# A two-layer transformer kernel whose matrix order is planned at build time: transposed P stored by layer in two halves, planner durations replaced, and the order written out anew

## The chip, the cores and the metric

The kernel runs on one core of one Trainium2 chip. A core has a matrix engine (TensorE, PE in the profile, with its weight loads shown apart as PEld), a vector engine (VectorE, DVE), a scalar engine (ScalarE, ACT), a general engine (GpSimd, POOL) and a queue engine (SyncE, SP) that starts most transfers. The metric is the device time of one execution in microseconds.

## What is computed

Two layers A and B are applied twice to x (2048 rows of 576, bf16). A is attention over segments of 32 rows with 8 memory rows that the segment before hands on, so its 64 segments are a chain; B is a gated feed-forward layer.

```python
for s in range(n_seg):                      # 64 segments, each needs mem of the one before
    h = concat([mem, xs])                   # 8 + 32 rows
    q, k, v = h @ Wq, h @ Wk, h @ Wv        # 576 -> 32 heads of 128
    p = softmax(where(mask, q @ k.T * scale, -1e9))
    o = (p @ v) @ Wo
    mem = o[:M]; outs.append(o[M:])
...
x = x + A(layernorm(x)); x = x + B(layernorm(x))     # B: (silu(x@w1) * (x@w3)) @ w2, 576 -> 4608 -> 576
x = x + A(layernorm(x)); x = x + B(layernorm(x))
```

## The kernel before, in words

The two applications of A run interleaved. Step t works on segment t of the first application and on segment t - 8 of the second (`LAG`), so that in the middle most matrix instructions serve both: 80 columns, 40 of each layer. There are 72 steps; the first 8 and the last 8 have one layer alone ("one-layer steps", 40 columns), and the 56 between have two. Every fourth step a feed-forward job of 128 rows per layer starts, whose pieces are laid between the attention work.

A step has four head groups g of 8 heads. For a group, TensorE's work is a chain of blocks, each with a letter in the written order:

- Q and q: queries and keys (32 matmuls over 128 rows of the contraction, and 8 short ones for its last 64 rows, the "tail"). ScalarE or VectorE moves the result from PSUM into tile QKT.
- S: scores. VectorE adds the mask, takes the maximum, subtracts, ScalarE takes the exponential (tile SME), VectorE sums, inverts and multiplies into tile PB (3 or 4 instructions).
- T: transposes P, 8 matmuls from PB through the small matrix `fold`, whose 320 result columns (8 heads by 40) are shared by both layers on different partitions. Two evictions then read the same PSUM bank whole and write tile PTS, one for each layer, each multiplied by a column of zeros and ones (`slots`) that keeps the partitions of its layer. Each goes to ScalarE or VectorE, as the planner chooses (`pt_ev`, line 1022). There is one PTS buffer.
- P: 8 matmuls, V by PTS, 80 columns each (`pv`, line 1039). It needs both evictions, and V. The result is moved to tile OT.
- O and o: output projection, 32 matmuls and 8 for the tail.
- V, v, X, x, G, g: values (memory rows, segment rows, and both of two steps at once), moved to tile V. F, f, W, w: the feed-forward blocks, up (16 and 4 matmuls) and down (8, w for the second layer). a, b, n, p, m: transposes.

The order of everything is fixed when the program is built. `make_nodes` makes one node for each block and each piece of work of another engine, with a duration in microseconds. `plan` (line 76) goes through them: TensorE takes its nodes exactly as the string `ORDER` says (line 222: `FIRST`, eleven times `FOUR`, `LAST`; `FOUR` is 4 steps and 224 letters), and the other engines take whichever ready node can begin first by the durations, which also decides between ScalarE and VectorE where a node may go to either ("AD"), and which PSUM bank and buffer it gets. Only the resulting order is emitted, each engine's instructions chained in that order; the durations are no part of the program. A node is ready some latency after its producers (`PE_LAT`, `EW_LAT`). The planner knows no dependence between the two evictions of one T: both wait for T alone (line 404).

TensorE blocks have modes: whole array ("full"), 64-column halves ("col", where each matmul is issued as two halves side by side, `mm`, line 586), and row or quarter modes for tails. Blocks that may run in either of two modes take that of their neighbours.

Of the kernel before, what the change touches and what calls it, by code (L numbers as in the profile page):

```python
# [13 lines left out]
P = 128  # L14
# [18 lines left out]
PE_LAT = 0.22  # L33
EW_LAT = 0.135
# [17 lines left out]
class Node:  # L52
# [3 lines left out]
    def __init__(self, eng, dur, fn, deps=(), prio=0.0, mode=None, acq=(), rel=(), name="", lat=None):  # L56
        self.eng, self.dur, self.fn, self.prio, self.mode = eng, dur, fn, prio, mode.split("/") if mode else mode
        self.deps = [d for d in deps if d is not None]
        self.acq, self.rel, self.name = list(acq), list(rel), name
        self.lat = lat if lat is not None else (PE_LAT if eng == "PE" else EW_LAT)  # L60
        self.outs, self.ready, self.start, self.end, self.by = [], 0.0, None, None, None
        self.left = len(self.deps)
# [13 lines left out]
def plan(nodes, pools, letters):  # L76
# [42 lines left out]
    while len(order) < len(nodes):  # L119
# [35 lines left out]
        for s in n.acq:  # L155
# [4 lines left out]
            f[s.i] = NOW  # L160
        for s in n.rel:
            s.users -= 1
            s.end = max(s.end, n.end + (PE_LAT if e == "PE" else EW_LAT))
            if s.users == 0:
                free[s.pool][s.i] = s.end
        for m in n.outs:
            m.ready = max(m.ready, n.end + (0.0 if m.eng == e == "PE" else n.lat))
# [8 lines left out]
def actc(*ns):  # L176

    return sum(max(0.067 + n * 0.000833, 0.19) for n in ns)


def dve(*ns):
    return sum(max(0.065 + n / 960.0, 0.19) for n in ns)


def dveh(*ns):

    return sum(max(0.065 + n / 1920.0, 0.19) for n in ns)
# [6 lines left out]
def ewh(*ns):  # L194
# [5 lines left out]
    "amQQQQqqqqSSqqQQQTSQqqSxXVvPTPTOPOOTooPoOoQQqqqqQSQvqqSVQQqTqSQPQOSToPXTOPTxoPOOooQqqqQQSVvqQQSQqqqQSqTQPOSTPTOP"  # L200
    "OToooPaOoQQqqqqQQSvSVQqqqQQQSqTPSXTOPTOPoTxoPOOooQQpQqqqvVqSnQQSFfqFQqfqqQTQSPFTfSOFPWOToPFToffPOOooWQqqqqQQSQQS"
    "FFfqfVvqTQWQqSFxffqQFPSXTWfPFTOPOTOPFOooooWQfqqqQQSFqfqVvQQSFfqTQPWQSqqfFTQOSfoPFTOPWFTOPooffOoFQqqQqqvSQQWSVqqf"
    "FQQWqqSTQPQSTOPabOTXPooTOPxxOooXqqpQQQqqSQnVvfSFTQqqqQQPSFffqQFTOPoSWTFfPOOTFPWOooofQQqfqqFSQFqqfgQGWTQPQSfqFQQq"
    "fqFSWTGFSggfGPGTOPOTfgFaPOOooooWVvqqfQQFFQSqfqQWQSqqfFQTQQqfqSFPWTSFPOTfoOPFWTOPffFOoooWQQqqqqQSbQQQqgqSGSTGPQTq"
    "gqQPOggSGTGPOTOPoooOoQqqqpQVpSQnQvqqqQnQFSTffqFQQPqSwTFPSffOOWTFPFTOPWOoooowFffqqQQQWSfqqFQwQSFqfqgGTQQPWfqSTFFg"
    "gfqGQwPGTOoSPFgfOGTOPWOoooFqqfqQQQQvSwqVSFqqfQQWwTFPQfqfqFTQSwPWSfFOTFPWwOTffFPOOaooooWQQqqqqQwSbQGQgqqSQTQPQqqg"
    "SGTSGPGggTOPOTOPoooOo"
# [5 lines left out]
LAST = (  # L213
    "QqqqpQQQSnpQQqqqVSvTSnQFffqPFOQqTwPoSWTFPffFTOOWPwOoooFFqfqQQQqqfSQQwQfqqFTSGSqfgQFPWQgfqGTSFPGFTfggOOPGTOPwWOoo"
    "ooFFqffqQQwQWQSqqVSvqqQQTFQPSfqqQwTOWSPFTFPofOTOPwOoooWFfqfqQQQQqfqSFwWvVSFTfqqQQPWQqqSvTQVSPOTbOPwOTooPoxOoXqQp"
    "pVvQqqqQSQQnqqSQnqQFTSfqQPFTSOPfTFOPwTOPWOooooFqfqfQQQSVqqqvQQQwSfqFWTFPSfqqQTQOPSFTwfFPOTOPWOooooFfqqQQQSqfxvVX"
    "qfFQwWTSQFQqqqfQPWSTwFPffqQFTWSOwFPffOFTOPwOooooWFvqfqQQQSWqqVQwSFfqqfQFTQQSqqWPQTPSOoTOPwOToobPxOoXqqqQQQpvSVqQ"
    "qQSnqQFfSTQFPqqfQOTSFfPwTOoofPFTOPFOfoowQqqQFSQfqqqQQSVvqqfQFTQFSfqPQOTowPSFTfxXPOTOPFOooowVvqqQQQSqqfQQSqqfQFST"
    "QQPwqqFTSOfPFTOfPwTOPfoooOoFQQqqqqQSQQSqqQVvSfTFPqQQwqfTSFPOTOFPTOPfoooOoFpwnfffFFwFwfffFFFwfffFFwFwfffFFFwfffFF"
# [12 lines left out]
def make_nodes(em, nseg, pools, o=Opt, dma_bw=230e3, load_bw=400e3):  # L232
# [44 lines left out]
    def ln_nodes(tag, src, xn, deps, prio, writes, warm=False):  # L277

        a = node("DVE", 1.16, em.ln_stats(src, xn), deps=deps, prio=prio, acq=[] if src is xn else [xn], name=tag + "stats")
        p_ = node("POOL", 0.45, em.ln_pow(xn), deps=[a], prio=prio, name=tag + "pow")  # L280
        c = node("DVE", 0.46 if src is xn else 0.66, em.ln_norm(src, xn), deps=[p_], prio=prio, name=tag + "norm")
# [28 lines left out]
    def v_nodes(name, t, k, prio, tail_at, emit, strips, deps, tail_deps, free):  # L310
# [6 lines left out]
        for r in (0, 1):  # L317
            outs = em.v_parts(strips, r)
            b[r].users = len(outs)
            for p0, width, row, blk in outs:  # L320
                e = node("AD", (0.55, 0.6), em.v_ev(b[r], p0, width, row, blk), deps=[m_, n] + free.get(blk // 2, []), prio=prio + 0.01 * (blk // 2),
# [19 lines left out]
    def vg_out(t, g, b, deps, row):  # L341

        return [node("AD", (0.55, 0.6), em.v_ev(b[r], row, R64, row, 2 * g + r), deps=deps, prio=t + o.vm + 0.01 * g + (0.05 if row == 0 else 0.0), rel=[b[r]],
# [11 lines left out]
    def step(t):  # L355
# [17 lines left out]
        for g in range(NG):  # L373
# [18 lines left out]
            sc = node("PE", 8 * (0.0165 * nl if nl == 2 else 0.029), em.scores(t, g, qs, s), deps=qe, prio=pf + o.sc, mode="col" if nl == 2 else "full/col", acq=[s, sme], rel=qs, name="SC")  # L392
            a = node("DVE", dve(320), em.sm_add(t, g, s, sme), deps=[sc], prio=pf, rel=[s], name="add")
            m_ = node("DVE", dve(320, 320) + 0.13, em.sm_max(t, g, sme), deps=[a], prio=pf, name="maxsub")
            c = node("ACT", 0.105 + 320 * 0.000833, em.sm_exp(t, g, sme), deps=[m_], prio=pf, name="exp")
            pb = Slot("pb")
            d = node("DVE", dve(320) + 0.2, em.sm_sum(t, g, sme), deps=[c], prio=pf, name="sum")
            w = 0.168 * (4 - e if nl == 2 else 2) + nl * 320 / 960
# [954 lines left out]
```

## Time and profile before

| | |
|---|---|
| time of 3 runs, median (lowest to highest) | 2731.85 us (2730.61 to 2734.94) |
| span of the profiled execution, first to last instruction | 2722.1 us |
| median of the runs less that span | 9.75 us |
| granted TensorE clock, mean over the span | 0.996 |
| VectorE busy | 2115.9 us, 78% |
| ScalarE busy | 1377.2 us, 51% |
| GpSimd busy | 333.4 us, 12% |
| transfers | 322.07 MB, mean 118 GB/s |

The profiled execution's own time outside the span is not recorded, so sums below are made on the span, and the 9.75 us are added at the end. In the profile a row of a group reads: line, engine, operation, tile written <- tiles read, shape, count | busy us, mean ns of one | idle us of that engine just before them, and who ended it. Busy is the union of the bars; a matmul's bar is much longer than the distance to the next matmul, since they are pipelined. Line 591 is the helper that records every matmul, 594 ScalarE's, 597 VectorE's. A row of the timeline reads: start us, length us, engine, line, operation, tiles, shape, count, and in brackets the idle time before it and what ended it.

### The profile page before, as it was taken

The page shows a single profiled execution, that of the slowest core. Times are in us where ns is not written, and L with a number is a line of the kernel's source. Part 1 is how long each engine was busy: PE and PEld are TensorE (multiplying, and loading weights), DVE is VectorE, ACT ScalarE, POOL GpSimd, SP SyncE. Part 2 cuts the span into 40 slices and gives each one's busy share as a digit, 9 for nine tenths or more (in the row PEclk, how much of TensorE's full clock was granted, in tenths as well). Part 3 has the DMA queues.
Part 4 walks back from the last instruction along what each step waited for, and adds up shares of the span by engine and source line. Part 5 has one row for each costly group of instructions (what it writes and reads, how often), then busy time and mean ns, then how long its engine had stood idle before and what let it go on. Part 6 is the DMA issues. An engine that isn't in the chain of part 4 may idle for free.

```text
span 2722.1 us, 136659 instructions
## 1 busy us (share of the span) xinstructions
PE 2629.0 (97%) x60933; PEld 2278.8 (84%) x60933; DVE 2115.9 (78%) x5487; ACT 1377.2 (51%) x3914; POOL 333.4 (12%) x411
## 2 busy tenths in 40 slices
PE   5999999999999999999999999999999999999998
PEld 4788888888888888888888888888888888888886
DVE  5787887887778778777877877787787778687876
ACT  2655554454545455454545545454454545455453
POOL 1111110110111011011101101110110111011110
PEclk8999999999999999999999999999999999999999
DMA  9064524343342334434233433423344342434457
GB/s 314 5 183 122 151 73 126 88 118 116 103 124 84 109 96 118 116 100 124 86 110 96 118 116 98 125 85 111 97 118 116 98 125 71 124 97 121 125 172 252
DMA packets 478176, 322.07 MB, mean 118 GB/s; under 512 B 26024, under 2 KB 467760, under 8 KB 476944
## 3 DMA queue, kind: packets, MB, share of 16 engines
q1 hardware_dynamic: 474048, 305.43, 37.9%
q8 instruction: 477, 7.82, 1.2%
q0 software_dynamic: 3024, 6.93, 0.9%
q10 hardware_dynamic: 512, 0.94, 0.2%
q14 instruction: 115, 0.94, 0.1%
HBM read 308.49 MB, written 2.36 MB: 114 GB/s over the span
## 4 chain that ended last, share of the span: by engine, by line
PE 78%; DVE 10%; ACT 6%; DMA 2%; issue 2%; SPq 1%; ACTq 0%; DVEq 0%
PE bank L591 78%; DVE HTT L597 3%; ACT PTS L594 2%; DVE PTS L597 2%; DVE STAT L597 2%; DVE PB L597 2%; ACT V L594 2%; SPq L600 1%; DVE V L597 1%; DVE SME L597 1%; DMA W<-in_A_Wk_dram 1%; ACT SME L594 1%; DMA W<-in_B_w_dram 1%; DMA WO<-in_A_Wo_dram 0%; ACT QKT L594 0%
## 5 line engine op out<-in xcount | busy, mean ns | idle before, releaser
L591 PEld LDWEIGHTS <-W 128*128 128x128 bf16 (+2 forms) x32064 | 1266.0, 100 | 124.6 <-issue 60.2
L591 PE MATMUL bank<-HT,W 128*128 128x80 bf16 (+3 forms) x23040 | 807.6, 197 | 18.5 <-ACT HT L594 5.7
L591 PE MATMUL bank<-XTB,W 128*64 128x256 bf16 (+5 forms) x9024 | 664.0, 263 | 5.7 <-DMA W<-in_B_w_dram 2.8
L594 ACT ACTIVATE QKT<-bank 128x64 bf16<-128x64 f32 (+2 forms) x1476 | 342.5, 314 | 354.9 <-PE bank L591 350.1
L1010 POOL MEMSET PB<- 128x1024 bf16 x288 | 273.9, 951 | 1922.6 <-PE bank L591 1649.7
L591 PE MATMUL bank<-OT,WO 128*128 128x80 bf16 (+3 forms) x11520 | 409.7, 198 | 4.6 <-ACT V L594 2.2
L591 PEld LDWEIGHTS <-WO 128*128 128x128 bf16 (+1 forms) x11520 | 379.6, 102 | 29.9 <-issue 17.5
L594 ACT ACTIVATE V<-bank 32x512 bf16<-32x512 f32 (+1 forms) x613 | 344.4, 585 | 101.8 <-PE bank L591 94.8
L591 PE MATMUL bank<-WV,HT 128*32 128x512 bf16 (+4 forms) x3680 | 375.8, 381 | 2.1 <-DVE OT L597 0.9
L591 PE MATMUL bank<-W2C,HTT 128*64 128x288 bf16 (+1 forms) x3040 | 320.5, 286 | 2.0 <-DMA W2C<-in_B_w_dram 1.3
L597 DVE TENSOR_REDUCE STAT<-SME 104x8 f32<-104x320 f32 (+1 forms) x576 | 274.5, 477 | 35.1 <-ACT SME L594 29.4
L597 DVE TENSOR_TENSOR PB<-SME,STAT 40x128 bf16<-40x128 f32 (+4 forms) x912 | 274.4, 335 | 9.0
L594 ACT ACTIVATE HTT<-bank 128x512 bf16<-128x512 f32 (+1 forms) x324 | 177.5, 557 | 183.6 <-PE bank L591 182.4
L591 PEld LDWEIGHTS <-HT 128*32 128x32 bf16 (+4 forms) x3680 | 157.1, 99 | 122.0 <-issue 21.0
L591 PEld LDWEIGHTS <-HTT 128*64 128x64 bf16 (+1 forms) x3104 | 227.7, 104 | 35.5 <-issue 2.3
L597 DVE SCALAR_TENSOR_TENSOR XR<-bank,XR 128x288 f32<-128x288 f32 x576 | 239.6, 446 | 13.5 <-PE bank L591 11.6
L597 DVE CAST QKT<-bank 128x192 bf16<-128x192 f32 (+4 forms) x572 | 154.5, 316 | 121.2 <-PE bank L591 120.4
L597 DVE SCALAR_TENSOR_TENSOR HTT<-HTT,bank 128x512 bf16<-128x512 bf16 (+1 forms) x324 | 201.9, 623 | 52.5 <-ACT HTT L594 48.0
L594 ACT ACTIVATE PTS<-bank,slots 128x320 bf16<-128x320 f32 x303 | 151.0, 525 | 163.0 <-PE bank L591 113.7
L597 DVE TENSOR_TENSOR HTT<-HTT,bank 128x512 bf16<-128x512 bf16 (+1 forms) x324 | 203.6, 628 | 29.0 <-DVE HTT L597 0.9
L594 ACT ACTIVATE OT<-bank 128x320 bf16<-128x320 f32 (+1 forms) x402 | 149.6, 403 | 137.7 <-PE bank L591 132.2
L594 ACT ACTIVATE SME<-SME 104x320 f32<-104x320 f32 (+1 forms) x288 | 135.0, 469 | 156.3 <-DVE SME L597 154.5
(69 smaller groups left out, 1847.0 us busy)
## 6 DMA issues: line engine op xcount, KB each, us to landing
W<-in_B_w_dram SPq DMA_DIRECT2D x612, 256.0 KB, 3.6
W2C<-in_B_w_dram SPq DMA_DIRECT2D x306, 288.0 KB, 3.2
W<-in_B_w_dram SPq DMA_DIRECT2D x612, 32.0 KB, 3.2
W<-in_B_w_dram SPq DMA_DIRECT2D x8, 1024.0 KB, 11.9
W<-in_A_Wq_dram SPq DMA_DIRECT2D x9, 512.0 KB, 9.2
WO<-in_A_Wo_dram SPq DMA_DIRECT2D x4, 1152.0 KB, 16.7
XR<-in_A_x_dram POOLq DMA_DIRECT2D x16, 288.0 KB, 3.4
WV<-in_B_w_dram SPq DMA_DIRECT2D x4, 1152.0 KB, 11.2
```

The costliest lines, as they stand in the source:

```text
L591: self.ch("PE", self.nc.tensor.matmul(out, lhsT=lhsT, rhs=rhs, start=start, stop=stop, skip_group_check=True, **k))
L594: self.ch("ACT", self.nc.scalar.activation(*a, **k))
L597: self.ch("DVE", getattr(self.nc.vector, fn_)(*a, **k))
L600: self.ch("SP", self.nc.sync.dma_start(out=out, in_=in_))
L1010: return lambda n: self.ch("POOL", self.nc.gpsimd.memset(self.T.PB[:, pb.i], 0.0))
```

## The change

Three things are edited together.

1. **Layout of PTS.** Before, each head had 80 neighbouring columns, 40 of each layer, so an eviction wrote 8 runs of 40. Now the tile is two halves of 320, one for each layer. An eviction writes 320 neighbouring columns, and P's moving operand for a head is two runs of 40 that lie 320 apart. One-layer steps use the first half alone, as before.
2. **Durations and latencies of the planner.** The latency after a node is 0.205 (TensorE), 0.165 (ScalarE), 0.14 (VectorE) instead of 0.22 and 0.135 for all others; ScalarE's and VectorE's durations lose their floor of 0.19 and some constants change; the two-layer PTS eviction is 0.425 on ScalarE and 0.46 on VectorE, where it was about 0.33 and 0.40.
3. **The three strings of the order** are all different. They have the same lengths and the same letters in total.

```diff
-PE_LAT = 0.22
-EW_LAT = 0.135
+LATS = {"PE": 0.205, "ACT": 0.165, "DVE": 0.14, "POOL": 0.04}
...
-    return sum(max(0.067 + n * 0.000833, 0.19) for n in ns)
+    return sum(0.05 + n / 1200 for n in ns)
...
-    return sum(max(0.065 + n / 960.0, 0.19) for n in ns)
+    return sum(0.065 + n / 960 for n in ns)
...
 FOUR = (
-    "QvqqpQQpQqqVSSnnQQFqfqfFQTQfqqWSFPwTFPSfOOTFPwTOPWOooooFffqqQQQQqqSWFSFffqgGQTQPQQgqqqGSwTFPGSfgfgFTGOPOWTOPwOoo"
-    "ooFqqQQQQqfqVvSSwWFfqfqQQTFWQwQSFffqqFPWTOPSowTFPffOTOFPWwOoooFqqfqQQQWQSqqqaQSQQbQqgqSGTSGPgTGPOTggOPGTOPwOoooo"
+    "QqqpQQpQqqVvnSSnQFfqfqFQQQTfqqSFPWTFPSwTfFOOPWTwPOOooooFqqffQQQQfqqSFGSgqfFTQQPwQTQqqqgGSWPFGSfggfFOTGPOwTOPWOoo"
+    "ooFqfqqQQwWQQVqvSaSFFffqqQQwQQqqSTWSFPffTFOPWwTOFPffTOFPwWOooooFfqqQQWQQSqqqQSQQbQqgqSTGGPSgTGPOTggGPOTwPOOoooo"
 )
...
-            m_ = node("DVE", dve(320, 320) + 0.13, em.sm_max(t, g, sme), deps=[a], prio=pf, name="maxsub")
+            m_ = node("DVE", 0.912 if nl == 2 else 0.89, em.sm_max(t, g, sme), deps=[a], prio=pf, name="maxsub")
...
-            w = 0.168 * (4 - e if nl == 2 else 2) + nl * 320 / 960
+            w = (1.074 if e else 1.143) if nl == 2 else 0.466
...
-            node("POOL", 1.2, em.pb_zero(pb), deps=[tr], prio=pf, rel=[pb], name="pbz")
-            pe_ = [node("AD", ew(4 * c80), em.pt_ev(t, g, m, bt, pts), deps=[tr], prio=pf, rel=[bt], name="PTe") for m in (0, 1)]
+            node("POOL", 0.95, em.pb_zero(pb), deps=[tr], prio=pf, rel=[pb], name="pbz")
+            pe_ = [node("AD", (0.425, 0.46) if nl == 2 else ew(160), em.pt_ev(t, g, m, bt, pts), deps=[tr], prio=pf, rel=[bt], name="PTe") for m in (0, 1)]
...
-                self.cp(n, self.T.PTS[:, pts.i, m * w:(m + 1) * w], src[:, m * w:(m + 1) * w])
+                self.cp(n, self.T.PTS[:, pts.i, 0, m * w:(m + 1) * w], src[:, m * w:(m + 1) * w])
                 return
-            dst = self.T.PTS[:, pts.i, :].rearrange("p (h n) -> p h n", h=GH)[:, :, m * QW:(m + 1) * QW]
+            dst = self.T.PTS[:, pts.i, m, :]
...
-                        self.T.PTS[:, pts.i, j * nq:(j + 1) * nq], True, True)
+                        self.T.PTS[:, pts.i, 0:nq // QW, j * QW:(j + 1) * QW], True, True)
...
-    T.PTS = sp.tile([P, pools["pts"], GH * 2 * QW], BF, name="PTS")
+    T.PTS = sp.tile([P, pools["pts"], 2, GH * QW], BF, name="PTS")
```

The order of the built program, read before any run of it, shows 410 matmuls and as many weight loads fewer (60523 for 60933): blocks that ran in 64-column halves and now run whole. The other engines have the same work, with 64 instructions more on ScalarE and as many fewer on VectorE.

More of the change, by code (lines that the diff above doesn't have):

```diff
@@ L59, in __init__ @@
         self.acq, self.rel, self.name = list(acq), list(rel), name
-        self.lat = lat if lat is not None else (PE_LAT if eng == "PE" else EW_LAT)
+        self.lat = lat
         self.outs, self.ready, self.start, self.end, self.by = [], 0.0, None, None, None
@@ L160, in plan @@
             f[s.i] = NOW
+        late = LATS.get(e, 0.135) if n.lat is None else n.lat
         for s in n.rel:
             s.users -= 1
-            s.end = max(s.end, n.end + (PE_LAT if e == "PE" else EW_LAT))
+            s.end = max(s.end, n.end + late)
             if s.users == 0:
@@ L166, in plan @@
         for m in n.outs:
-            m.ready = max(m.ready, n.end + (0.0 if m.eng == e == "PE" else n.lat))
+            m.ready = max(m.ready, n.end + (0.0 if m.eng == e == "PE" else late))
             m.left -= 1
@@ L176, in actc @@
 def actc(*ns):
-    return sum(max(0.067 + n * 0.000833, 0.19) for n in ns)
+    return sum(0.05 + n / 1200 for n in ns)
 def dve(*ns):
-    return sum(max(0.065 + n / 960.0, 0.19) for n in ns)
+    return sum(0.065 + n / 960 for n in ns)
 def dveh(*ns):
-    return sum(max(0.065 + n / 1920.0, 0.19) for n in ns)
+    return sum(0.065 + n / 1920 for n in ns)
 def ew(*ns):
@@ L199 @@
 FIRST = (
[L200 to L204, printed above, removed]
@@ L277, in ln_nodes @@
     def ln_nodes(tag, src, xn, deps, prio, writes, warm=False):
-        a = node("DVE", 1.16, em.ln_stats(src, xn), deps=deps, prio=prio, acq=[] if src is xn else [xn], name=tag + "stats")
-        p_ = node("POOL", 0.45, em.ln_pow(xn), deps=[a], prio=prio, name=tag + "pow")
-        c = node("DVE", 0.46 if src is xn else 0.66, em.ln_norm(src, xn), deps=[p_], prio=prio, name=tag + "norm")
+        a = node("DVE", 1.157, em.ln_stats(src, xn), deps=deps, prio=prio, acq=[] if src is xn else [xn], name=tag + "stats")
+        p_ = node("POOL", 0.55, em.ln_pow(xn), deps=[a], prio=prio, name=tag + "pow")
+        c = node("DVE", 0.535 if src is xn else 0.698, em.ln_norm(src, xn), deps=[p_], prio=prio, name=tag + "norm")
         b = Slot("bank", users=len(writes))
@@ L320, in v_nodes @@
             for p0, width, row, blk in outs:
-                e = node("AD", (0.55, 0.6), em.v_ev(b[r], p0, width, row, blk), deps=[m_, n] + free.get(blk // 2, []), prio=prio + 0.01 * (blk // 2),
+                e = node("AD", (0.49, 0.6), em.v_ev(b[r], p0, width, row, blk), deps=[m_, n] + free.get(blk // 2, []), prio=prio + 0.01 * (blk // 2),
                          rel=[b[r]], name=name + "e")
```

43 lines of the change are left out of this document (24 added, 19 removed).

## The prediction

> **What bounds the kernel now.** I begin with the head of the page and the chain that ended last.
>
> ```profile
> span 2722.1 us, 136659 instructions
> PE 2629.0 (97%) x60933; PEld 2278.8 (84%) x60933; DVE 2115.9 (78%) x5487; ACT 1377.2 (51%) x3914; POOL 333.4 (12%) x411
> ...
> PE 78%; DVE 10%; ACT 6%; DMA 2%; issue 2%; SPq 1%; ACTq 0%; DVEq 0%
> ```
>
> TensorE is busy 97% and is most of the chain. So the end is set by TensorE's work plus the places where it waits for a result of VectorE or ScalarE. The change takes next to nothing from the work; it can win or lose only in the waits. The stages come next: the first 60 us, the rest of `FIRST`, the eleven repetitions of `FOUR`, and `LAST` (columns: window, us, busy us and count by engine, granted clock, DMA share, GB/s).
>
> ```profile
> 0.00:60.00 60.00, 31.77 (x783) 23.85 (x783) 28.60 (x73) 14.47 (x41) 11.57 (x34) 0.89 1.01 352
> 60.00:535.49 475.49, 457.67 (x11734) 393.17 (x11729) 378.71 (x1008) 251.24 (x750) 65.31 (x75) 0.99 0.38 108
> 535.49:2284.82 1749.33, 1718.40 (x38192) 1499.92 (x38192) 1376.22 (x3553) 897.69 (x2509) 203.14 (x241) 1.00 0.37 107
> 2284.82:2722.10 437.28, 421.18 (x10232) 361.84 (x10231) 332.39 (x854) 213.84 (x618) 53.42 (x62) 1.00 0.48 145
> ```
>
> The first 60 us wait for weights (DMA share 1.01), and the change does not touch that. A repetition takes 1749.33 / 11 = 159.0 us, of which TensorE is idle (1749.33 - 1718.40) / 11 = 2.8 us. That understates the waits, because a bar outlasts the distance to the next matmul:
>
> ```profile
> L591 PE MATMUL bank<-OT,WO 128*128 128x80 bf16 x7168 | 291.2, 202 | 2.5 <-ACT V L594 2.2 <-issue 0.3
> L591 PE MATMUL bank<-OT,WO 128*128 128x40 bf16 x2048 | 62.2, 181 | 1.1 <-DMA WO<-in_A_Wo_dram 0.6 <-ACT OT L594 0.5
> ```
>
> An 80-column matmul follows the last one after 291.2 / 7168 = 0.041 us, but its bar is 0.202 us, so each wait hides 0.16 us under a bar. Measured start to start, with each block's length when nothing is late, a repetition has 21 waits over 0.04 us, together 5.3 us: before P 2.1, before T 1.45, before S 0.6, before O 0.35, the rest 0.8. (The bound from the window is 2.8 + 21 x 0.16 = 6.2.) The end of a repetition shows the last of the 21 and how such waits come about:
>
> ```profile
> 842.00 1.31 PE L591 MATMUL bank<-OT,WO 128*128 128x80 bf16 x32 [0.20 <-ACT V L594]
> 843.14 0.36 PE L591 MATMUL bank<-fold,PB 104*128 104x40 bf16 x8
> 843.83 0.53 DVE L597 TENSOR_SCALAR PTS<-bank,slots 128x320 bf16<-128x320 f32 x1
> 844.39 0.53 ACT L594 ACTIVATE PTS<-bank,slots 128x320 bf16<-128x320 f32 x1 [0.83 <-DVE PTS L597]
> 845.56 0.47 ACT L594 ACTIVATE SME<-SME 104x320 f32<-104x320 f32 x1
> 846.06 0.49 DVE L597 TENSOR_REDUCE STAT<-SME 104x8 f32<-104x320 f32 x1 [0.98 <-ACT SME L594]
> 848.42 0.35 PE L591 MATMUL bank<-fold,PB 104*128 104x40 bf16 x8 [0.64 <-DVE PB L597]
> 848.62 1.31 PE L591 MATMUL bank<-OT,WO 128*128 128x80 bf16 x32
> 848.81 0.53 ACT L594 ACTIVATE PTS<-bank,slots 128x320 bf16<-128x320 f32 x1 [0.62 <-PE bank L591]
> 849.37 0.55 DVE L597 TENSOR_SCALAR PTS<-bank,slots 128x320 bf16<-128x320 f32 x1 [0.37 <-ACT PTS L594]
> 849.98 0.45 PE L591 MATMUL bank<-PTS,V 128*128 128x80 bf16 x8
> ```
>
> Two mechanisms stand here. **The pair of evictions is serial.** VectorE's eviction begins when ScalarE's has ended (848.81 + 0.53, then 849.37), so from T's end at 848.62 to P at 849.98 it takes 1.36 us. One block O lies between, worth 843.14 - 842.00 = 1.14 us, so 0.22 us is lost with no idle time in the row. **A serial pair also blocks a queue.** At 844.39 ScalarE had waited 0.83 us for VectorE's half; the exponential behind it began at 845.56, VectorE's sum waited 0.98 us for that, and T waited 0.64 us plus the part under a bar, 0.81. Over the whole run the pair makes its engines wait as in the first two rows; the third is T's visible idle time for PB:
>
> ```profile
> DVE PTS L597 <- ACT PTS L594: 56.2, 106, 2.1
> ACT PTS L594 <- DVE PTS L597: 30.2, 44, 1.9
> PE bank L591 <- DVE PB L597: 14.7, 29, 0.9
> ```
>
> **The change part by part.**
>
> *Does the layout make the pair parallel?* I take it that it does not. One-layer steps already write two separate stretches of PTS, and the second eviction waits for the first there too (12.6 us in the third row):
>
> ```profile
> L594 ACT ACTIVATE PTS<-bank,slots 128x320 bf16<-128x320 f32 x303 | 151.0, 525 | 163.0 <-PE bank L591 113.7 <-DVE PTS L597 25.9 <-ACT HTT L594 10.2
> L597 DVE TENSOR_SCALAR PTS<-bank,slots 128x320 bf16<-128x320 f32 x145 | 78.8, 544 | 46.9 <-ACT PTS L594 43.6 <-PE bank L591 1.4
> L597 DVE CAST PTS<-bank 128x160 bf16<-128x160 f32 x35 | 10.9, 322 | 18.1 <-ACT PTS L594 12.6 <-PE bank L591 5.4
> L594 ACT ACTIVATE OT<-bank 128x320 bf16<-128x320 f32 x297 | 122.2, 439 | 111.1 <-PE bank L591 106.6 <-DVE STAT L597 1.0
> L597 DVE CAST OT<-bank 128x320 bf16<-128x320 f32 x151 | 73.6, 487 | 43.3 <-PE bank L591 41.2 <-ACT OT L594 0.6
> L594 ACT ACTIVATE QKT<-bank 128x256 bf16<-128x256 f32 x331 | 128.7, 398 | 147.9 <-PE bank L591 145.5 <-ACT QKT L594 0.8
> L594 ACT ACTIVATE OT<-bank 128x160 bf16<-128x160 f32 x105 | 27.4, 302 | 26.6 <-PE bank L591 25.6
> ```
>
> What both halves share is the PSUM bank they read. The order of the changed program, with the semaphores that each instruction waits for, still holds one eviction back for the other in 132 of its 133 two-layer pairs that are split between the engines (142 of 143 before). The Trainium skill (PSUM — Partial Sum Buffer, "PSUM bank collisions raise a hardware error") says why no layout of the destination would do: two engines must not touch one bank and the same 32 partitions at once, reads against reads included. The rows agree as far as they go; by that rule this part is worth nothing.
>
> *Does it make an eviction shorter?* PTS takes 525 ns on ScalarE where OT, as large, takes 439; on VectorE 544 and 487. The 86 and 57 ns are the most that contiguous writing can give; the least is nothing. OT's line, (439 - 302) / 160 = 0.856 ns a column, gives 384 ns at 256 columns, and QKT, which writes those in 4 separate runs, takes 398: 14 ns for 4 runs. So runs are cheap, and I take 0 as the nearest. (The other end: 0.14 us off a split pair, at some 5 tight places a repetition and 0.14 x 5 x 11 = 8 us in all.) The Trainium skill (ScalarE: Activation LUTs, "What ACT_TABLE_LOAD costs") puts about 93 ns on each per-partition pointer operand, which the scale `slots` is and which the change keeps; by that all of the 86 ns stays.
>
> *P's moving operand in two runs.* No matmul of the trace reads such an operand. At most a break costs what two 40-column matmuls cost over one of 80: 2 x 62.2 / 2048 - 291.2 / 7168 = 20 ns, for 224 x 8 = 1792 two-layer matmuls 36 us; at least nothing. The instructions stay as many and the columns too, so I take nothing, nearest to the 80-column row, and keep the 36 us as a rival.
>
> *Fewer halves.* 410 pairs of half-width matmuls become single ones:
>
> ```profile
> L591 PE MATMUL bank<-W2C,HTT 128*128 128x288 bf16 x1440 | 203.9, 286 | 1.8 <-DMA W2C<-in_B_w_dram 1.3 <-DVE HTT L597 0.5
> L591 PE MATMUL bank<-W2C,HTT 128*64 128x288 bf16 x1600 | 116.6, 287 | 0.1
> ```
>
> A pair costs 2 x 116.6 / 1600 = 0.146 us, one 203.9 / 1440 = 0.142; 410 x 0.004 = 1.7 us less.
>
> *The order and the durations* are the change proper, and here it is counted what lies between. **Before P.** In the old `FOUR` five T have a lone O or Q before their P (1.14 us against a need of up to 1.36); they and two P that also wait for V make the 2.1 us. In the new `FOUR` "TOP" stands once and "TwP" twice; all three pairs are split. A w is worth 8 x 0.142 = 1.14, less where it overlaps the next mode: read start to start 0.98. So 0.22 + 2 x (1.36 - 0.98) = 0.98 us remains. That is 1.1 us less a repetition, and shows that the new order lays P closer than the pair allows. **Before T.** The 0.81 us shown goes: in the new order of ScalarE that exponential stands ahead of the eviction that blocked it. The second largest, in the second step, last group, is here:
>
> ```profile
> 769.64 0.36 PE L591 MATMUL bank<-fold,PB 104*128 104x40 bf16 x8 [0.34 <-DVE PB L597]
> ...
> L597 DVE CAST V<-bank 64x512 bf16<-64x512 f32 x145 | 99.2, 685 | 5.3 <-PE bank L591 2.1
> ```
>
> It loses 0.34 + 0.16 = 0.5 us. Between this group's mask and its PB VectorE had, among others, one eviction of PTS, one of V, and one of OT that the new order puts elsewhere (544 + 685 + 487 ns = 1.7 us), with the same 8.2 us of TensorE's work between S and T. So it goes too: together 1.3 us. **Before S and O** there is 0.95 us, of which half may go, 0.5. In all 2.9 of 5.3 us could go in a repetition. But a wait that goes brings the next one forward, and the pairs that the planner takes for parallel still block the queues: I let a third come back. That is 1.9 us x 11 = 21 us. `FIRST` after 60 us and `LAST` are 475.5 + 437.3 = 913 us, 5.7 repetitions, but part of their waits is for loads and the closing job; I take half the rate, 1.0 x 5.7 = 6 us.
>
> *SP's and POOL's queues* carry the same transfers in another order. The nearest that two uses of a weight buffer come is 4.8 us of TensorE's work in the old repetition and 5.0 in the new one, over the 3.6 us below; the cover holds, and costs nothing.
>
> ```profile
> W<-in_B_w_dram SPq DMA_DIRECT2D x612, 256.0 KB, 3.6
> ```
>
> Sum: 21 + 6 + 1.7 = 29 us off the span: 2722.1 - 29 = 2693. The median of the runs is 2731.85 - 2722.1 = 9.75 above the span, which gives **2703 us**.
>
> **The rivals.**
>
> *All of it goes.* If nothing comes back and the small waits shrink too, 4 us a repetition and 2 elsewhere: 44 + 11 + 2 = 57 us, 2675. For it: both T's have clear causes. Against it: 132 serial pairs remain.
>
> *Slower: the split pair.* The new order has 28 two-layer P with less than 1.0 us of work after T, where the old has 3; each costs 0.38 us when its pair is split, 25 x 0.38 = 9.5 us more. Places with one O (1.0 to 1.3 us) fall from 69 to 21, which is 48 x 0.22 = 10.5 us less. So P brings nothing, and what decides is the queues behind the pair: if each repetition gets one more blocked exponential like the 0.81 us shown than it loses, it is 0.81 x 11 = 9 us slower, 2741; with the T waits only coming back elsewhere it is no change. The point is that the waits before T grow instead of shrinking.
>
> *Slower: the broken operand.* At the full 20 ns, 2703 + 36 = 2739; break-even is 29 / 1792 = 16 ns a matmul. Against it: a matmul's pitch follows its columns, and these stay.
>
> *The pair does run side by side after all.* Then T to P needs 0.19 + 0.55 + 0.05 = 0.8 us, the three places cost nothing, and 0.98 x 16 = 15 us more go: 2688. The built order speaks against it.
>
> **How the numbers follow.** Measurement can tell about 0.2% of this kernel, 5.5 us, from no change. Forecast, 2685 to 2722: 0.57 (side by side, 0.02, lies in it). All of it: 0.16. No change, 2726 to 2737: 0.09, as a mixture of gains and the split pair. Slower by the split pair 0.11, by the broken operand 0.07. So faster 0.73, same 0.09, slower 0.18. The range reaches from just above the best case to the far end of the second and third rivals: 2678 to 2742.
>
> **What would show it right or wrong.** In the repeated stage TensorE's idle time falls from 2.8 to about 1.5 us a repetition, and a repetition from 159.0 to 157.1 us. VectorE's and ScalarE's waits for each other's PTS stay near 56 and 30 us; if they vanish, the pair is parallel. PTS evictions stay near 525 and 544 ns. P's matmuls keep their distance; if it grows to 50 ns or more, the broken operand is real. T's idle time for PB, 14.7 us over the run, halves; if it does not, the forecast's main step is wrong.

## The result, and the profile after

The changed kernel takes 2706.44 us, median of 4 runs (2704.38 to 2709.95), against 2731.23 (2728.40 to 2734.94) for the kernel before in the same measurement: a ratio of 0.9917, 95% interval 0.9903 to 0.9932. The forecast was 2703 us, faster. The sign and the size of the change came out about as forecast, a fall of 24.8 us where 29 were expected; two terms of the sum did not, and they cancel each other in part.

The head of the changed kernel's page and its chain of waits:

```profile
span 2705.0 us, 135792 instructions
PE 2618.6 (97%) x60482; PEld 2272.3 (84%) x60523; DVE 2097.7 (78%) x5423; ACT 1401.6 (52%) x3978; POOL 334.1 (12%) x411
...
PE 80%; DVE 9%; ACT 6%; issue 2%; DMA 2%; SPq 1%; POOL 0%; ACTq 0%; DVEq 0%; POOLq 0%
```

TensorE's share of the chain rises by two points, VectorE's falls by one. The stages of the changed kernel (columns as in the prediction's table of stages):

```profile
0.00:60.00 60.00, 32.70 (x760) 23.26 (x762) 28.73 (x74) 14.72 (x39) 11.57 (x34) 0.91 1.01 351
60.00:532.41 472.41, 455.43 (x11714) 390.01 (x11710) 372.15 (x993) 256.29 (x765) 65.89 (x75) 1.00 0.39 108
532.41:2260.46 1728.05, 1707.41 (x37863) 1497.60 (x37896) 1365.27 (x3498) 917.88 (x2564) 203.65 (x242) 1.00 0.38 108
2260.46:2705.00 444.54, 423.06 (x10161) 361.48 (x10162) 331.56 (x859) 212.67 (x613) 52.95 (x61) 1.00 0.48 142
```

The repeated stage falls from 1749.33 to 1728.05 us, 159.0 to 157.1 a repetition. What lies before it falls from 535.49 to 532.41. `LAST` grows, from 437.28 to 444.54. Together -21.3 - 3.1 + 7.3 = -17.1 us, which is the difference of the two spans.

Read start to start as in the prediction (a block's distance to the next, less what the same two blocks take when nothing is late, added up over the eleven repetitions), the waits of the repeated stage are:

| waits before, us in 11 repetitions | kernel before | changed kernel |
|---|---|---|
| P | 23.6 | 19.0 |
| T | 16.5 | 0.8 |
| S and O | 11.1 | 3.2 |
| Q, q, G | 2.5 | 12.9 |
| all | 58.5 | 37.5 |

The table of waits of the changed kernel (who waited <- for whom: us in total, times, longest us) shows T's part at once, and the split pair unchanged:

```profile
DVE PTS L597 <- ACT PTS L594: 53.5, 93, 2.5
ACT PTS L594 <- DVE PTS L597: 24.4, 42, 1.1
PE bank L591 <- ACT PTS L594: 12.3, 20, 1.9
PE bank L591 <- DVE PTS L597: 5.4, 20, 1.0
PE bank L591 <- DVE PB L597: 2.6, 8, 0.5
PE bank L591 <- DVE XN L597: 1.9, 1, 1.9
```

T's idle time for PB was 14.7 us and is 2.6. The engines still wait 53.5 and 24.4 us for each other's half of PTS, and TensorE 12.3 + 5.4 us for the last half (5.4 + 4.6 in the kernel before). The timeline of the changed kernel shows one of the two "TwP" of a repetition; here and below, only the rows of the blocks and evictions that are spoken of are shown:

```profile
722.30 0.36 PE L591 MATMUL bank<-fold,PB 104*128 104x40 bf16 x8
722.50 1.14 PE L591 MATMUL bank<-W2C,HTT 128*128 128x288 bf16 x8
722.70 0.53 ACT L594 ACTIVATE PTS<-bank,slots 128x320 bf16<-128x320 f32 x1 [1.39 <-PE bank L591]
723.26 0.55 DVE L597 TENSOR_SCALAR PTS<-bank,slots 128x320 bf16<-128x320 f32 x1 [0.72 <-ACT PTS L594]
723.86 0.45 PE L591 MATMUL bank<-PTS,V 128*128 128x80 bf16 x8 [0.22 <-DVE PTS L597]
```

The w behind T starts at 722.50, and P comes 1.36 us later. That w covers 0.98 of it; 0.38 is lost, just as counted before the run. The other one, in the repetition's last step, is worse:

```profile
841.00 1.21 ACT L594 ACTIVATE V<-bank 64x512 bf16<-64x512 f32 x2
841.37 0.36 PE L591 MATMUL bank<-fold,PB 104*128 104x40 bf16 x8
841.48 0.67 DVE L597 CAST V<-bank 64x512 bf16<-64x512 f32 x1
841.58 1.14 PE L591 MATMUL bank<-W2C,HTT 128*128 128x288 bf16 x8
842.18 0.55 DVE L597 TENSOR_SCALAR PTS<-bank,slots 128x320 bf16<-128x320 f32 x1
842.77 0.53 ACT L594 ACTIVATE PTS<-bank,slots 128x320 bf16<-128x320 f32 x1 [0.56 <-DVE PTS L597]
843.35 0.45 PE L591 MATMUL bank<-PTS,V 128*128 128x80 bf16 x8 [0.63 <-ACT PTS L594]
```

Here both engines were busy with evictions of V when T ended, VectorE until 842.15 and ScalarE until 842.21. VectorE took the first half, and ScalarE stood idle for 0.56 us until it was done. P came 1.77 us after T's end, and 0.79 was lost: the pair began late and ran one after the other.

### The profile page after: what moved, and what is told of

Read it like the earlier page. It is cut to its first block, busy times and chain, and to the rows that moved or that the text cites. A ratio compares the mean times of both kernels' runs of the same rounds, so it can differ in the third digit from the quotient of the medians.

```text
span 2705.0 us, 135792 instructions
## 1 busy us (share of the span) xinstructions
PE 2618.6 (97%) x60482; PEld 2272.3 (84%) x60523; DVE 2097.7 (78%) x5423; ACT 1401.6 (52%) x3978; POOL 334.1 (12%) x411
## 4 chain that ended last, share of the span: by engine, by line
PE 80%; DVE 9%; ACT 6%; issue 2%; DMA 2%; SPq 1%; POOL 0%; ACTq 0%; DVEq 0%; POOLq 0%
PE bank L591 80%; ACT V L594 3%; DVE STAT L597 2%; DVE PTS L597 2%; ACT PTS L594 1%; DVE V L597 1%; DVE SME L597 1%; DVE PB L597 1%; DMA W<-in_A_Wk_dram 1%; DVE HTT L597 1%; SPq L600 1%; DMA W<-in_B_w_dram 1%; ACT HT L594 0%; ACT QKT L594 0%; DMA WV<-in_A_Wv_dram 0%
## 5 line engine op out<-in xcount | busy, mean ns | idle before, releaser
L594 ACT ACTIVATE QKT<-bank 128x256 bf16<-128x256 f32 (+2 forms) x1524 | 349.5, 311 | 363.5 <-PE bank L591 320.7
L591 PE MATMUL bank<-OT,WO 128*128 128x80 bf16 (+2 forms) x11520 | 401.6, 198 | 2.2 <-issue 1.8
L591 PE MATMUL bank<-WV,HT 128*32 128x512 bf16 (+5 forms) x3728 | 362.3, 381 | 3.8 <-issue 2.2
L591 PE MATMUL bank<-W2C,HTT 128*128 128x288 bf16 (+1 forms) x2776 | 318.4, 286 | 2.9 <-issue 1.8
L591 PEld LDWEIGHTS <-HT 128*32 128x32 bf16 (+4 forms) x3768 | 164.1, 99 | 119.5 <-issue 20.3
L591 PEld LDWEIGHTS <-HTT 128*128 128x128 bf16 (+1 forms) x2840 | 222.4, 103 | 42.2 <-issue 4.5
L597 DVE CAST QKT<-bank 128x192 bf16<-128x192 f32 (+4 forms) x524 | 140.5, 315 | 117.7 <-PE bank L591 117.3
L594 ACT ACTIVATE PTS<-bank,slots 128x320 bf16<-128x320 f32 x315 | 157.0, 531 | 128.8 <-PE bank L591 95.0
```

Of the source, the lines that this page charges most:

```text
L591: self.ch("PE", self.nc.tensor.matmul(out, lhsT=lhsT, rhs=rhs, start=start, stop=stop, skip_group_check=True, **k))
L594: self.ch("ACT", self.nc.scalar.activation(*a, **k))
L597: self.ch("DVE", getattr(self.nc.vector, fn_)(*a, **k))
```

## The experiments

Each kernel differs from the changed kernel or from the one before only as shown. Four later measurements of the kernel before gave medians of 2724.1 to 2724.8 us. So kernels are compared by their ratio to the kernel before; 0.9917 is some 2701.5 us there. The theory at the start was that the new strings bring the gain by themselves, that the layout brings nothing, and that the serial pair is what is left. In the diffs, dots stand for further lines.

**The layout, taken out of the change and put alone into the kernel before.**

```diff
...
-            dst = self.T.PTS[:, pts.i, m, :]
+            dst = self.T.PTS[:, pts.i, :].rearrange("p (h n) -> p h n", h=GH)[:, :, m * QW:(m + 1) * QW]
+            src = src.rearrange("p (h n) -> p h n", h=GH)
...
-                        self.T.PTS[:, pts.i, 0:nq // QW, j * QW:(j + 1) * QW], True, True)
+                        self.T.PTS[:, pts.i, j * nq:(j + 1) * nq], True, True)
...
-    T.PTS = sp.tile([P, pools["pts"], 2, GH * QW], BF, name="PTS")
+    T.PTS = sp.tile([P, pools["pts"], GH * 2 * QW], BF, name="PTS")
```

> The changed kernel with PTS laid out as before (80 columns a head), new order and new durations kept. Theory (the gain is the new order's, in the waits before T, S and O; the layout gives nothing): 2706 us, within 3. Rival (the layout shortens the evictions or frees the pair): over 2710; if the pair's serial wait had gone with the layout, the three tight P of a repetition would cost 1.4 us more here, 15 us, 2721.

The second kernel has the reverse of this diff on the kernel before.

> The kernel before with the new layout of PTS alone, old order and old durations. Theory: 2731 us, within 3. Rival (the layout gives part): 2727 or less. If two runs of 40 columns in P's operand cost anything, over 2734.

Measured: without the layout 0.9915 (0.9901 to 0.9929), the layout alone 0.9997 (0.9987 to 1.0006). The layout is worth nothing that can be measured. The groups of the kernel with the layout alone say why:

```profile
L594 ACT ACTIVATE PTS<-bank,slots 128x320 bf16<-128x320 f32 x303 | 151.0, 525 | 162.0 <-PE bank L591 112.9 <-DVE PTS L597 26.0 <-ACT HTT L594 11.2
L597 DVE TENSOR_SCALAR PTS<-bank,slots 128x320 bf16<-128x320 f32 x145 | 78.9, 545 | 46.0 <-ACT PTS L594 42.7 <-PE bank L591 1.3
L591 PE MATMUL bank<-PTS,V 128*128 128x80 bf16 x1232 | 69.6, 200 | 12.0 <-ACT V L594 3.5 <-ACT PTS L594 3.2 <-DVE PTS L597 1.0
```

The evictions take 525 and 545 ns (525 and 544 with the runs of 40), VectorE still waits 42.7 us for ScalarE's half, and a block of eight matmuls of P, now with an operand in two runs, takes 69.6 x 8 / 1232 = 0.452 us. In the kernel before, with one run, the same 1232 matmuls take 69.7 us:

```profile
L591 PE MATMUL bank<-PTS,V 128*128 128x80 bf16 x1232 | 69.7, 201 | 12.2 <-ACT V L594 3.4 <-ACT PTS L594 3.2 <-DVE PTS L597 1.4
```

**The strings alone, and the durations alone**, each in the kernel before, with the layout of before.

> The kernel before with the three new strings alone: TensorE's order is exactly the changed kernel's, but the old durations choose which engine takes an eviction, in which order VectorE and ScalarE work, and which bank is used. Theory: what TensorE has between S and T and between T and P carries most of the gain, 2706 to 2715. Rival (TensorE's order and the other engines' order gain only together): over 2722.

> The kernel before with the new durations and latencies alone, old strings and old layout: TensorE's order is the old one, the other engines' order and the engine of an eviction are chosen by the new durations. Theory: the old string keeps its tight places, 2725 to 2737. Rival (the better choice of engines is what gained): 2715 or less.

Measured: strings alone 1.0214 (1.0198 to 1.0231), durations alone 1.0054 (1.0039 to 1.0070). Each makes the kernel slower, the durations alone by more than was expected, and both together make it 0.9915. My theory that the strings do it by themselves has fallen. Where the strings alone lose shows in TensorE's waits of that kernel:

```profile
PE bank L591 <- DVE XN L597: 29.1, 13, 3.7
PE bank L591 <- DVE PB L597: 18.6, 28, 3.1
```

The changed kernel waits for XN once, 1.9 us, and 2.6 us for PB. XN is the layer norm that VectorE makes for the next job. VectorE's order is no part of the strings: the planner lays it by its durations, and by the old ones the same string finds the layer norm late, 24.3 us of start-to-start waits in the repeated stage. Which of the numbers the strings depend on is asked further down.

**The pair's serial rule told to the planner.** The program stays as it is; the planner lets the second eviction of a bank begin only when one of another engine has ended.

```diff
+        self.read = {}
...
+        for s in n.rel:
+            if s.pool == "bank" and e in ("ACT", "DVE"):
+                for x, end in s.read.items():
+                    if x != e:
+                        t = max(t, end)
...
+            if s.pool == "bank" and e in ("ACT", "DVE"):
+                s.read[e] = n.end + late - 0.035
```

> The changed kernel, same strings and durations, but its planner knows that two evictions of one PSUM bank on different engines run one after the other, and so chooses engines anew. Theory (what the new order still loses before P is the serial split pair): far fewer pairs are split, VectorE's and ScalarE's waits for each other's PTS (53.5 and 24.4 us) fall below half, the P waits of the repeated stage (19 us) fall by 5 or more, and the time to 2698 to 2704 against 2706 for the changed kernel. Rival (the split pair costs nothing that something else would not take): 2705 or more.

And the simplest way to have no split two-layer pair, both evictions on ScalarE:

```diff
-            pe_ = [node("AD", (0.425, 0.46) if nl == 2 else ew(160), em.pt_ev(t, g, m, bt, pts), deps=[tr], prio=pf, rel=[bt], name="PTe") for m in (0, 1)]
+            pe_ = [node("ACT" if nl == 2 else "AD", 0.425 if nl == 2 else ew(160), em.pt_ev(t, g, m, bt, pts), deps=[tr], prio=pf, rel=[bt], name="PTe") for m in (0, 1)]
```

> The changed kernel with both evictions of a two-layer T given to ScalarE. No pair is split, so the two waits for each other's PTS go to nearly nothing (one-layer steps alone). Theory: T to P needs 1.2 us instead of 1.4, the three tight places lose 0.5 us less in a repetition or more, but ScalarE has 133 more evictions of 0.43 us: 2700 to 2706. Rival: ScalarE's longer queue costs as much as is won, 2706 to 2720.

Measured: 0.9883 (0.9868 to 0.9898) and 0.9883 (0.9866 to 0.9899), both 156.61 us a repetition. Against 2731.23 us that is 2699, within what was expected of the rule and 1 us below what was expected of ScalarE alone. With the rule VectorE's waits for ScalarE's half are gone from the table of waits, and ScalarE's for VectorE's half fall from 24.4 to 2.2 us. The waits before P in the repeated stage fall from 19.0 to 9.9 and 7.0 us. The timeline of the kernel with the rule shows the same "TwP" as above, its pair now on one engine:

```profile
720.78 0.36 PE L599 MATMUL bank<-fold,PB 104*128 104x40 bf16 x8
720.99 1.14 PE L599 MATMUL bank<-W2C,HTT 128*128 128x288 bf16 x8
721.18 0.94 ACT L602 ACTIVATE PTS<-bank,slots 128x320 bf16<-128x320 f32 x2 [1.15 <-PE bank L599]
722.18 0.45 PE L599 MATMUL bank<-PTS,V 128*128 128x80 bf16 x8
```

P comes 1.19 us after T's end instead of 1.36. The stages of this kernel from the repeated one on:

```profile
531.49:2254.22 1722.73, 1709.45 (x37863) 1497.73 (x37895) 1350.12 (x3465) 929.05 (x2597) 205.88 (x242) 1.00 0.37 108
2254.22:2692.80 438.58, 420.80 (x10161) 360.99 (x10162) 328.86 (x852) 215.03 (x620) 52.64 (x60) 0.99 0.48 143
```

With the same strings `LAST` is back from 444.54 to 438.58 us. So its loss in the changed kernel was not the string's alone.

**T into two banks, one for each eviction.** T is issued twice; both engines may then read at once.

```diff
...
-            bt = Slot("bank", users=2)
+            bt = [Slot("bank"), Slot("bank")] if nl == 2 else [Slot("bank", users=2)]
...
-            for j in range(GH):
-                self.mm(self.bk(b)[:, j * QW:(j + 1) * QW], self.T.PB[0:104, pb.i, j, :], self.T.fold[0:104, :], True, True)
+            for x in b:
+                for j in range(GH):
+                    self.mm(self.bk(x)[:, j * QW:(j + 1) * QW], self.T.PB[0:104, pb.i, j, :], self.T.fold[0:104, :], True, True)
```

> The changed kernel with T of the two-layer steps issued twice, into two PSUM banks, one for each eviction; nothing else is changed, and what is computed is the same. It is not meant to be fast: 224 x 8 more matmuls of 25 ns are 45 us, and a bank more is held. Theory (the shared bank makes the pair serial): VectorE's wait for ScalarE's PTS and the reverse fall from 53.5 and 24.4 us to a few us, of the one-layer steps. Rival (the shared PTS tile makes it serial): they stay. Time by the first count 2750 or more.

Measured: 1.0128 (1.0107 to 1.0148). The timeline, the groups and one row of the waits of this kernel:

```profile
722.34 0.80 PE L591 MATMUL bank<-fold,PB 104*64 104x40 bf16 x32
722.98 0.53 ACT L594 ACTIVATE PTS<-bank,slots 128x320 bf16<-128x320 f32 x1 [1.35 <-PE bank L591]
...
723.24 0.55 DVE L597 TENSOR_SCALAR PTS<-bank,slots 128x320 bf16<-128x320 f32 x1
```

```profile
L591 PE MATMUL bank<-fold,PB 104*128 104x40 bf16 x3144 | 119.2, 180 | 23.6 <-DVE HTT L597 20.7 <-DVE PB L597 2.1 <-DVE SME L597 0.2
L591 PE MATMUL bank<-fold,PB 104*64 104x40 bf16 x1904 | 43.4, 186 | 1.6
L597 DVE TENSOR_SCALAR PTS<-bank,slots 128x320 bf16<-128x320 f32 x174 | 93.9, 540 | 4.1 <-PE bank L591 2.0
```

```profile
DVE PTS L597 <- ACT PTS L594: 11.1, 19, 1.4
```

With two banks the evictions overlap (723.24 is before 722.98 + 0.53), and VectorE's idle time before its half is 4.1 us in all. In the changed kernel it is 41.0:

```profile
L594 ACT ACTIVATE PTS<-bank,slots 128x320 bf16<-128x320 f32 x315 | 157.0, 531 | 128.8 <-PE bank L591 95.0 <-DVE PTS L597 23.7 <-ACT V L594 7.1
L597 DVE TENSOR_SCALAR PTS<-bank,slots 128x320 bf16<-128x320 f32 x133 | 73.2, 550 | 41.0 <-ACT PTS L594 38.9 <-PE bank L591 0.6
L591 PE MATMUL bank<-fold,PB 104*128 104x40 bf16 x1816 | 82.2, 180 | 2.8 <-DVE PB L597 2.3 <-POOL PB L1010 0.2
L591 PE MATMUL bank<-fold,PB 104*64 104x40 bf16 x976 | 27.7, 186 | 0.1
```

VectorE's waits for ScalarE's half fall from 53.5 to 11.1 us, all before the 128x160 evictions of one-layer steps, which still share a bank; ScalarE's waits for VectorE's half fall from 24.4 to 0.6. PTS and its layout are the same in both kernels, so it is the shared bank that makes the pair serial. The second set of transposes keeps TensorE busy for (119.2 + 43.4) - (82.2 + 27.7) = 52.7 us more, and the profiled spans differ by 2759.8 - 2705.0 = 54.8.

**Strings for the mended rule.** The planner with the serial rule, and three strings searched anew under it by the planner's own reckoning; the diff shows `FOUR`.

```diff
-    "QqqpQQpQqqVvnSSnQFfqfqFQQQTfqqSFPWTFPSwTfFOOPWTwPOOooooFqqffQQQQfqqSFGSgqfFTQQPwQTQqqqgGSWPFGSfggfFOTGPOwTOPWOoo"
-    "ooFqfqqQQwWQQVqvSaSFFffqqQQwQQqqSTWSFPffTFOPWwTOFPffTOFPwWOooooFfqqQQWQQSqqqQSQQbQqgqSTGGPSgTGPOTggGPOTwPOOoooo"
+    "QQpQqqqqQpvVnSSQnQFfqqfFTQQfqqSFPWTFPSwfTOFPOTwWPOOooooFqfqfQQqqQQSFSfgqfFGTQwPQQQgqqqGSWTFPGSfggfFOTGPOTWwPOOoo"
+    "ooFfqqvVQWQQQfqqwSFSFfqqqQQQWwTQfqfSaPFTSFPOWTOwFPffTFPOwOoooWoFqqfqQQWQQSqqqQSQQbQqqgTSGGPSgTGPOggTGPOTOPwOoooo"
```

> The planner of the run in which the serial pair is known, with three strings that were searched anew under that rule (same letters, other places). Theory, that strings and durations gain only when they are made for each other: the strings of the change were searched while the planner took the pair for parallel, so under the mended rule there must be better ones. In the run with the serial pair known the repeated stage still had 32.2 us of waits; I expect a repetition to fall from 156.6 to about 155.3 us, FIRST and LAST together to give some 5 us, and a median of 2670 to 2682 for 2693. Rival, that the changed strings are as good as any and what is left are latencies that no order hides: within 5 us of 2693.

Measured: 2669.78 us, 0.9799 (0.9785 to 0.9814): faster than both kernels, by 0.0084 x 2724 = 23 us than the same planner with the changed strings, in the expected 2670 to 2682 but for 0.2 us. The rival falls. What the run does not separate is the rule from a second search: no run has strings searched again without the rule. The planner's own count speaks for the rule. It is no measurement, but the time at which TensorE's last block ends in the plan: 2601.9 us for the changed strings and 2630.4 for these by the changed kernel's planner, and 2627.0 and 2602.4 with the rule. The stages of this kernel from the repeated one on:

```profile
527.13:2232.37 1705.24, 1697.76 (x38060) 1490.14 (x38104) 1354.81 (x3487) 917.78 (x2575) 203.04 (x241) 1.00 0.37 109
2232.37:2666.40 434.03, 419.75 (x10149) 361.37 (x10149) 327.89 (x850) 216.32 (x622) 53.71 (x62) 0.99 0.48 146
```

A repetition takes 1705.24 / 11 = 155.0 us; its waits are 16.2 us in eleven repetitions (1.8 of them before P), against 37.5 (19.0).

**What the scaling column costs.**

```diff
-                self.act(dst, src, ACT.Copy, scale=keep)
+                self.act(dst, src, ACT.Copy)
             else:
-                self.v("tensor_scalar", dst, src, keep, None, op0=ALU.mult)
+                self.v("tensor_copy", dst, src)
```

> The changed kernel with the two-layer PTS evictions as plain copies: the multiplication by the column of zeros and ones is left out, so that each half of PTS holds the rows of both layers (the computation is changed there). It measures what a scaling column costs. By the first rival of the eviction's length, that the gap to OT comes from this operand: ScalarE's 531 ns fall to about 440 and VectorE's 550 to about 490, and T to P is some 0.09 to 0.15 us shorter in each split pair; at some 5 tight places a repetition up to 8 us, a median of 2697 to 2706. By the other, that the gap belongs to writing PTS at all: 525 and 545 ns stay, and so does 2706.

Measured: 0.9862 (0.9847 to 0.9877), some 15 us below the changed kernel by the ratios, and 20.4 by the spans of the two profiled executions. The groups of this kernel:

```profile
L594 ACT ACTIVATE PTS<-bank 128x320 bf16<-128x320 f32 x315 | 129.2, 444 | 123.9 <-PE bank L591 94.1 <-DVE PTS L597 19.9 <-ACT V L594 7.1
L597 DVE CAST PTS<-bank 128x320 bf16<-128x320 f32 x133 | 65.0, 489 | 32.9 <-ACT PTS L594 28.5 <-PE bank L591 0.6
```

531 becomes 444 ns and 550 becomes 489. The whole gap between PTS and OT belongs to the operand and none of it to the runs of the destination. The repeated stage gains what was expected, 8.2 us (157.10 to 156.35 a repetition); what lies before it gains 6.4 and `LAST` 5.8 beside, which I had not counted, and the total is beyond the expected range. Part of these two may be the scatter of single executions, which the table further down shows.

**Which of the planner's numbers.** Three times one group is put back in the changed kernel: the PTS durations; the latencies; the durations of the scores and the softmax chain.

```diff
-            pe_ = [node("AD", (0.425, 0.46) if nl == 2 else ew(160), ...
+            pe_ = [node("AD", (0.334, 0.398) if nl == 2 else ew(160), ...
```

```diff
-LATS = {"PE": 0.205, "ACT": 0.165, "DVE": 0.14, "POOL": 0.04}
+LATS = {"PE": 0.22}
```

```diff
...
-            m_ = node("DVE", 0.912 if nl == 2 else 0.89, em.sm_max(t, g, sme), deps=[a], prio=pf, name="maxsub")
+            m_ = node("DVE", dve(320, 320) + 0.13, em.sm_max(t, g, sme), deps=[a], prio=pf, name="maxsub")
...
-            w = (1.074 if e else 1.143) if nl == 2 else 0.466
+            w = 0.168 * (4 - e if nl == 2 else 2) + nl * 320 / 960
...
```

> The changed kernel with one duration put back: the planner takes 0.334 us on ScalarE and 0.398 us on VectorE for a two-layer PTS eviction, as before, where the change has 0.425 and 0.46. It asks whether the gain hangs on these two numbers or on the other durations and latencies. If on these, most of the 25 us goes and the waits before P grow by 10 us or more in the repeated stage: 2715 to 2730. If strings and the whole set of durations hang together only through the other engines' queues, a small change of the set already shuffles them: some 5 to 15 us slower, 2711 to 2721, with the loss spread over T, S and QK. If neither matters, 2706 within 5.

> The changed kernel with one group of the planner's numbers put back: the latencies (0.22 us after TensorE, 0.135 us after every other engine). With both PTS durations put back nothing was lost, so the dependence of the strings on the planner must sit in other numbers. If it sits in the latencies, which stand behind every node, the gain goes and the waits spread over all blocks: a repetition of 158.5 to 160 us and 2725 to 2745. If it sits in the softmax chain, this run stays at 2706 within 5 and the other of this pair loses.

> The changed kernel with the other group put back: the planner's durations of the scores and of the softmax chain between S and T (maximum and subtraction, exponential, sum, the multiplication into PB, PB's own latency). If the strings hang on these, the waits before T come back and VectorE's queue is shuffled: 2720 to 2745, more of it in FIRST and LAST than in the repeated stage. If they hang on the latencies alone, 2706 within 5. If both groups lose about the whole gain each, then any large group of wrong numbers is enough, and the gain belongs to no single number.

Measured, with all kernels beside each other (stages from the profiled executions; start is all before the repeated stage):

| kernel | ratio | start | a repetition | LAST |
|---|---|---|---|---|
| before | 1 | 535.5 | 159.03 | 437.3 |
| changed | 0.9917 | 532.4 | 157.10 | 444.5 |
| layout alone | 0.9997 | 537.9 | 159.01 | 439.8 |
| changed, old layout | 0.9915 | 530.5 | 157.24 | 444.1 |
| strings alone | 1.0214 | 546.6 | 161.49 | 456.3 |
| durations alone | 1.0054 | 539.6 | 159.41 | 448.3 |
| changed, old PTS durations | 0.9925 (0.9909 to 0.9942) | 531.2 | 157.27 | 442.5 |
| changed, old latencies | 1.0059 (1.0036 to 1.0081) | 535.2 | 160.36 | 438.7 |
| changed, old softmax | 1.0020 (1.0010 to 1.0029) | 549.4 | 157.41 | 450.0 |
| serial rule known | 0.9883 | 531.5 | 156.61 | 438.6 |
| both on ScalarE | 0.9883 | 525.7 | 156.61 | 439.9 |
| two banks | 1.0128 | 533.4 | 161.92 | 445.3 |
| serial rule, new strings | 0.9799 | 527.1 | 155.02 | 434.0 |
| no scaling column | 0.9862 | 526.0 | 156.35 | 438.7 |

Before and layout alone run the same order, and so do the changed kernel and that with the old layout. Within these two pairs a repetition differs by 0.02 and 0.14 us, but the start by 2.4 and 1.9 and `LAST` by 2.5 and 0.4: outside the repeated stage, differences of 2 or 3 us between single executions say nothing.

The PTS durations matter nothing by themselves; a likely reason, not tested, is that a planner that takes the pair for parallel is wrong about its end with either. Either of the other two groups costs the whole gain and more, in different places. With the old latencies the loss is not spread over all blocks, as was expected; the layer norm is late again, in the repeated stage:

```profile
PE bank L591 <- DVE XN L597: 24.5, 12, 2.2
```

With the old softmax durations the repetition stays at 157.4 and the start loses 17 us, 9.6 of them in waits before T (14.3 for 4.7). So the third outcome of the last expectation holds: the gain is in the agreement of strings and numbers, not in one number. The planner's own count shows the same without the chip: for the strings before it gives 2627.0 us with the old numbers and 2640.7 with the new, for the changed strings 2706.3 and 2601.9. Each string does best with its own set of numbers.

## Why the prediction was right, and where it was wrong

*The layout makes nothing parallel: right.* 53.5 and 24.4 us of waiting for each other remain; two banks take VectorE's idle time before its half from 41.0 to 4.1 us. The Trainium skill's rule (PSUM — Partial Sum Buffer, "PSUM bank collisions raise a hardware error"), that two engines must not read one bank and the same 32 partitions at once, agrees with these numbers; here it is the program's order that holds one eviction back, and no run shows what two engines in one bank would do without it.

*The evictions are not shorter: right*, and now shown: the 86 and 57 ns of the bounds are the operand's 87 and 61.

*The broken operand of P costs nothing: right.* A block of eight takes 0.452 us with it. The 36 us rival is out.

*Fewer halves, 1.7 us:* not measured apart. *Queues of SP and POOL at nothing:* the stage after the loads and the repeated stage both became shorter, with 0.38 to 0.39 of DMA share where it was 0.37 to 0.38; no loss to a transfer stands out.

*The repeated stage, -21 us: right in sum,* -21.3, *and only in part by its terms.* T: 16.5 to 0.8 (forecast 1.6), as the mechanism says. S and O: 11.1 to 3.2 (forecast 5.0). "Let a third come back": 10.4 us came back, before Q, q and G, where 10.6 were forecast. P: of 23.6, 19.0 stay where 10.8 were forecast, among others because the second "TwP" costs 0.79 instead of 0.38. So P was mis-sized by 8.2 us of a gain of 21, and smaller waits elsewhere made up for it; that the sum agrees to 0.3 us is luck. TensorE's idle time is (1728.05 - 1707.41) / 11 = 1.9 us a repetition for 1.5 forecast; the trace lacks 41 matmul records (60482 for 60523 weight loads), which may account for some of the difference.

*`FIRST` and `LAST`, -6 us: wrong.* In the two profiled executions they gave -3.1 + 7.3 = +4.2. In the other pair of the same two orders, layout alone and old layout, they gave -7.4 + 4.3 = -3.1. So their sum is known only to several us, but both pairs fall short of the forecast, and in both `LAST` lost. This is the step that failed: "I take half the rate". `LAST` does not share the repeated stage's rate. With the serial rule known the same string takes 438.6 there, both evictions on ScalarE 439.9, without the scaling column 438.7: every edit that makes the pair cheaper or places it otherwise takes back 4 to 6 us. That points to the rival's mechanism, a split pair that blocks a queue, in the stage where I had not counted it. That the old latencies give 438.7 too, with the pair still split, says that it hangs on how the queues happen to fall and not on the pair's price alone; which block lost first there stays open.

*The 9.75 us on top of the span: wrong.* In the runs whose own span is recorded the time outside it is 1.7 us (up to 3.1). The profiled execution of before was some 8 us shorter than the median of its three runs; that scatter is not time outside the span. The span was forecast at 2693 and is 2705.0, 12 us more; the addition was 8 too large. That 2703 lies near 2706 is in part this cancellation. Of the 12 us, 10 are `FIRST` and `LAST`, with their scatter, and the rest is about the 1.7 of the halves. Against the ratio, -0.83% or 23 us, the sum of 29 was 6 too large.

*Why it worked at all:* the prediction credited the order. The runs say: order and durations together, neither alone (1.0214 and 1.0054). Counting what lies between blocks in the built order was sound, because the built order of every engine holds both.

## What to carry to other kernels

Where a planner lays the other engines by its durations, an order written for one engine belongs to these durations. Here the new strings with the old numbers lost, and so did the old strings with the new numbers. A correction that makes the model truer can still gain with the strings as they are (the serial rule, 0.9917 to 0.9883), and searching the order again under it gained more (0.9799). In this kernel two engines that evict one bank take turns, so leave both evictions on one engine or tell the planner. Forecast each stage from its own waits, and take the time outside the span from runs that record both, not from a median less another execution's span.

## What the runs showed of the hardware

A per-partition scaling column costs 87 ns on an eviction of 320 columns on ScalarE (531 to 444) and 61 on VectorE (550 to 489). The Trainium skill's figure (ScalarE: Activation LUTs, "What ACT_TABLE_LOAD costs"), about 93 ns for such an operand, fits the first. What the column is worth in this kernel, 15 us, was twice what the tight places count. Two evictions of one bank on ScalarE alone took 0.94 us (721.18 in the kernel with the rule; one alone takes 0.53, so the bars overlap); split over two engines they took 0.53 + 0.55 and a gap of 0.03 (722.70 in the changed kernel), with VectorE free when ScalarE ended. So here the split was the slower way, 1.36 us from T to P for 1.19.
